# Spectral filter and feed-forward kernel: batch 0's first transform stage from stationary x into on-chip memory, batch 1's y set up later, and the inverse stage's calls in pairs inside the feed-forward

## The chip, the cores and the metric

The kernel runs on one core of a Trainium2 chip. The metric is device time in microseconds (us) of one execution; three runs are shown for the kernel before, and one more execution was profiled. The engines are PE (matrix multiply; PEld is its weight load), DVE (vector), ACT (scalar), POOL and SP, whose queue issues all DMAs here.

## The reference, cut to what matters

```python
B, S, D, FF = 8, 3136, 256, 1024
X = rfft(x, axis=1)                          # along the 3136 positions
Yr = Xr @ w_r - Xi @ w_i + b_r
Yi = Xr @ w_i + Xi @ w_r + b_i
Y  = soft_threshold(Yr, 0.01) + 1j * soft_threshold(Yi, 0.01)
y  = irfft(Y, n=3136, axis=1)
h  = relu(y @ w_in)                          # (B, S, 1024)
c  = conv_w[0]*h[s-1] + conv_w[1]*h[s] + conv_w[2]*h[s+1]   # per channel
out = (h * sigmoid(c)) @ w_out               # (B, S, 256)
```

## The kernel before, in words

**Spectral part.** A transform of 3136 = 49 x 64 points is two short transforms. Stage 1 (`quarters`, L296 to L301) multiplies x by the 49-point table `f1`: the table is the stationary operand (49 x 64), x streams past it 512 columns at a time, and row halves and column halves of the array work at once, four matmuls to a call. For batch 0 this is `stage1_head` (L320): eight pieces of x are loaded, multiplied, copied out of PSUM by ACT and DVE (L330, L331) and stored to a scratch tensor in DRAM, `sc1` (`store_a1`, L307 and L308). `load_a2` (L339) reads them back in the layout of the next stage. The other batches' stage 1 (`stage1`) runs between the items below. Then come 50 items: six per batch, each of four of the 24 frequency groups, and two for the left-over frequency of four batches each. For an item, stage 2 (`stage2`, L354, into `ps_s2`) is the 64-point transform; `mix` (L382, into `ps_mx`) multiplies by the complex weights `wmix`, which are written as high and low fp32r parts (`split`, L188 and L189); `threshold` and `stage3` (L416) follow, and the result `z1` is stored to a second scratch tensor, `sc2` (L421). The loop over `it` at L496 interleaves stage 2 of item `it` with the mix of `it-1`, the threshold of `it-2` and stage 3 of `it-3`. In it the order on PE, DVE and ACT is the written one.

**Stage 4** (`stage4`, L136) is the last inverse transform. Eight calls make a batch's `y`, each from a loaded tile `z2` (L133): 32 small fp32 matmuls with `z2` (50 x 64) stationary and the table `i2` (49 columns) streaming (L144), then ACT writes the high part `yh` (L150) and DVE the low part `yl` (L152). A call's PSUM tile comes from the pool `psh`, which has two buffers and is shared with the feed-forward. Batch 0's eight calls are woven into the end of the spectral part (`to_y`).

**Feed-forward.** 28 column blocks (`ci`) of 2 x 448 positions by 8 channel groups (`f`) make 224 steps. Step `st` runs `up` (L599): 12 matmuls of 450 columns into a `psh` tile; then the chain relu (ACT, L601), first tap (ACT L606, or DVE L604 for `f` 0 and 4), two more taps (DVE, L608), sigmoid (ACT, L609), product (DVE, L610), high part `gh` (ACT, L613) and low part `gl` (DVE, L614). Four steps later `down` (L627) multiplies them by `w_out`: 21 matmuls of 256 columns. While a batch is in the feed-forward, the next batch's `y` is made: `new_y` (L155) takes the buffer `y_a` or `y_b` and clears its edge columns with four small DVE memsets (L159, L160), and the steps with `f` of 1, 4 and 7 each run one stage 4 call behind their `up`. In the feed-forward, the Tile scheduler and not the written order decides how the instructions of each engine are lined up. `y_b`, batch 1's buffer, lies where `z1` tiles lay, so its first use waits for their stores.

Of the kernel before, what the change touches and what calls it, by code (L numbers as in the profile page):

```python
# [9 lines left out]
F32 = mybir.dt.float32  # L10
# [90 lines left out]
def spectral_ffn_kernel(ctx: ExitStack, tc: tile.TileContext, x, w_r, w_i, b_r, b_i,  # L101
# [10 lines left out]

    i2 = cst.tile([P, 112], F32, name="i2")[:, 0:R]
    cw = cst.tile([P, 3, NF], F32, name="cw")
    win = [cst.tile([P, NT, FF], F32R, name=f"win_{q}") for q in range(2)]
    wout = [cst.tile([P, NF, D], F32R, name=f"wout_{q}") for q in range(2)]
    small = cst.tile([P, 32], F32, name="small")
    mlam, warm = small[:, 0:1], small[:, 1:2]

# [43 lines left out]
    with ExitStack() as late:  # L163
# [6 lines left out]
        pool("top", 1, late, side="right").tile([P, 80], F32, name="pad")  # L170
        cmx = late.enter_context(tc.tile_pool(name="cmx", bufs=1, side="right"))
        DB, XRB, SL_ENG = 1, 3, nc.gpsimd
        ps1 = ps_early.enter_context(tc.tile_pool(name="ps1", bufs=2, space=PSUM))
        ps2 = ps_early.enter_context(tc.tile_pool(name="ps2", bufs=2, space=PSUM))
        psa = late.enter_context(tc.tile_pool(name="psa", bufs=1, space=PSUM, side="right"))
        psm = late.enter_context(tc.tile_pool(name="psm", bufs=1, space=PSUM, side="right"))

        f1 = c1.tile([P, P], F32, name="f1")[:, 0:SP]
        t2 = c1.tile([KQ, U + 1, K2], F32, name="t2")
        cmx.tile([P, 72], F32, name="pad")  # L180
# [13 lines left out]
        def load_t2(g):  # L194
            sl = slice(g * UG, min((g + 1) * UG, U + 1))
            return nc.sync.dma_start(t2[:, sl, :], fwd2v[:, sl, :])

        def load_mix():

            raw = [stg.tile([P, NT, D], F32, name=f"wm_raw{k}", tag="raw", bufs=2) for k in range(2)]  # L200
            for k in range(2):
                ld = nc.sync.dma_start(raw[k], (w_r, w_i)[k].rearrange("(t p) e -> p t e", p=P))
            yield ld
            split(wmix_hi[:, :, 0, :], wmix_lo[:, :, 0, :], raw[1])
            for k, op in ((1, ALU.subtract), (2, ALU.add)):
                w = stg.tile([P, NT, D], F32, name="wm", tag="wm")
                nc.vector.tensor_tensor(w, raw[0], raw[1], op=op)
                split(wmix_hi[:, :, k, :], wmix_lo[:, :, k, :], w)
            yield None

# [50 lines left out]
        def later():  # L261
            nc.sync.dma_start(i2, inv2)
            bits = [load_bits(conv_w[k].rearrange("(f p) w -> p f w", p=P), NF, "cw") for k in range(2)]
            for k in range(3):
                top, rest = yield from from_bits(bits[k], NF, "cw")
                yield nc.vector.tensor_tensor(cw[:, k, :], top, rest, op=ALU.add)
                if k == 0:
                    bits.append(load_bits(conv_w[2].rearrange("(f p) w -> p f w", p=P), NF, "cw"))
            pieces = []
            for t in range(NT):  # L270
                for c in range(0, FF, WP):
                    pieces.append(([q[:, t, c:c + WP] for q in win], winv[:, t, c:c + WP, :], "win"))
            for f in range(0, NF, 2):
                pieces.append(([q[:, f:f + 2, :].rearrange("p a d -> p (a d)") for q in wout], woutv[:, f:f + 2, :, :], "wout"))
            asked = []
            for n in range(len(pieces) + 1):
                work = split_weight(*asked.pop(0)) if n else iter(())
                for _ in range(5):
                    if n:
                        yield next(work)  # L280
                if n < len(pieces):
                    dst, src, nm = pieces[n]
                    asked.append((dst, load_bits(src, WP, nm), WP, nm))
                    yield None
                yield from work
# [10 lines left out]
        def quarters(ps, xr):  # L296

            for c in range(2):
                for h in range(2):
                    rows = slice(h * SP, h * SP + R)  # L300
                    nc.tensor.matmul(ps[h][c * SP:(c + 1) * SP], f1[rows, :], xr[rows, 2 * c:2 * c + 2, :], start=True, stop=True)  # L301

        def store_a1(b, jc, a1):

            to = sc1[b].rearrange("(w h) (q c j) d -> q c w h j d", h=2, c=2, j=2)[jc]
            for c in range(2):
                nc.sync.dma_start(to[c, 0:R - 1], a1[c * SP:c * SP + R - 1])  # L307
            return nc.sync.dma_start(to[:, R - 1], a1[R - 1::SP])  # L308
# [11 lines left out]
        def stage1_head(xs, b=0):  # L320

            with tc.tile_pool(name="ha", bufs=1, side="right", reuse_waits="tile") as ha:
                for jc, xr in enumerate(xs):
                    a1 = ha.tile([P, 2, JC // 2, D], F32, name=f"ha{jc}")
                    if jc % 2:
                        ps = [psm.tile([P, JC // 2, D], F32, name="ps_s1h", tag=f"ps_mx{h}") for h in range(2)]
                    else:
                        ps = [ps1.tile([P, JC // 2, D], F32, name="ps_s1") for h in range(2)]
                    quarters(ps, xr)
                    nc.scalar.copy(a1[:, 0], ps[0])  # L330
                    nc.vector.tensor_copy(a1[:, 1], ps[1])  # L331
                    st = store_a1(b, jc, a1)
            return st

        def load_a2(b, g):
# [107 lines left out]
        with tc.tile_pool(name="hx", bufs=1, side="right", reuse_waits="tile") as hx:
            xh = []
            for p in range(NQ):
                xr, ld = load_x(hx, 0, p, tag=f"hx{p}")
                xh.append(xr)
            with tc.issue_after(ld.ins):
                mix_w = load_mix()
                next(mix_w)  # L450
                load_t2(0)
                with tc.manual_schedule(engines={mybir.EngineType.PE, mybir.EngineType.DVE, mybir.EngineType.Activation}):
                    st = stage1_head(xh)
                    next(mix_w)
        asked = []

        def ask():
            asked.append(load_x(s1p, *firsts[NQ + len(asked)], bufs=XRB)[0])
# [5 lines left out]
                    ask()  # L464

        first = halves()
        with tc.issue_after(st.ins):
            a2s[0], ld = load_a2(*items[0])
        with tc.issue_after(ld.ins):
            ask()  # L470
            load_bias()
            a2s[1], ld = load_a2(*items[1])
            for _ in range(2):
                ask()
        order.enter_context(tc.manual_schedule(engines={mybir.EngineType.PE}))
        order.enter_context(tc.issue_after(ld.ins))
        io, cab, wk, wkf = [pool(nm, n, late, side="right") for nm, n in (("io", 3), ("cab", 1), ("wk", 2), ("wkf", 2))]
# [18 lines left out]
        for it in range(n_it + 1):  # L496
# [153 lines left out]
    for st in range(n_st + LAG):  # L650
        if st < n_st:
            ci, f = divmod(st, NF)
            hv = [divmod(2 * ci + a, NH) for a in range(2)]
            if f == 0:
                nb = hv[1][0] + 1
                if nb < B and nb not in ys and hv[0][0] == hv[1][0]:
                    ys[nb] = new_y((y_a, y_b)[nb % 2])
                    todo = [(nb, jg) for jg in range(NPC)]
            gs[st] = up(f, [(ys[b], a * CH) for b, a in hv])
            if todo and f in (1, 4, 7):  # L660
                b, jg = todo.pop(0)
                for _ in stage4(load_z2(zio, b, jg), jg, ys[b], psh.tile([P, 2, 512], F32, name="ps_s4", tag="ps_h")):
                    pass
        if st >= LAG:
            ci, f = divmod(st - LAG, NF)
            accs = down(ci, f, gs.pop(st - LAG), accs)
# [24 lines left out]
```

## Time and profile before

| | |
|---|---|
| median of three runs | 1700.11 us (1698.52 to 1700.85) |
| profiled execution | 1701.23 us |
| its span | 1699.5 us |
| PE busy | 1652.3 us, 97% of the span |
| DVE busy | 1470.4 us, 87% |
| ACT busy | 1208.4 us, 71% |
| feed-forward starts | at about 507.6 us |

A busy PE is not PE at its peak: matmuls overlap, and their recorded durations are longer than the distance from one start to the next. So the distances between starts are what a step costs, and the gaps in PE's row of time are where an engine order or a wait costs something.

### The profile page before, as it was taken

To read this page: it belongs to the slowest core of one execution; us is meant where nothing else is said; L and a number is where in the kernel's file an instruction comes from. 1 tells how busy PE (TensorE), PEld (TensorE's weight loads), DVE (VectorE), ACT (ScalarE), POOL (GpSimd) and SP (SyncE) were. 2 spreads that over 40 slices of the span, in tenths; PEclk is the share of its full clock that TensorE was granted. 3 is DMA by queue.
4 is the path that set the end of the run, shared out by engine and by line. 5 is a ranking of instruction groups with operands and counts; after the bars stand their busy time and mean duration, and the time that the engine had idled before them with its cause. 6 is when DMAs were issued, how large, how long until landed. Compare 5 with 4: busy or idle time off the path is not lost.

```text
span 1699.5 us, 35829 instructions
## 1 busy us (share of the span) xinstructions
PE 1652.3 (97%) x15200; PEld 1517.6 (89%) x15200; DVE 1470.4 (87%) x1757; ACT 1208.4 (71%) x1615; POOL 119.2 (7%) x54
## 2 busy tenths in 40 slices
PE   4899999999998999999999999999999999999998
PEld 1688888889987999999999999999999999999998
DVE  2698999999987888888888888888888888888887
ACT  1677777787666776777777677777777777777676
POOL 0122222222220000000000000000000000000000
PEclk9999999999998999999999999999999999999999
DMA  8998879785542110111111011111101111000001
GB/s 202 252 273 274 253 222 280 241 249 185 163 137 62 49 51 22 52 51 43 49 51 46 22 52 52 42 52 51 43 23 52 52 42 52 23 23 23 22 23 44
DMA packets 143361, 165.91 MB, mean 98 GB/s; under 512 B 11745, under 2 KB 115169, under 8 KB 143201
## 3 DMA queue, kind: packets, MB, share of 16 engines
q1 hardware_dynamic: 143200, 163.63, 33.2%
q8 instruction: 119, 1.95, 0.5%
q14 instruction: 42, 0.34, 0.1%
HBM read 86.00 MB, written 77.59 MB: 96 GB/s over the span
## 4 chain that ended last, share of the span: by engine, by line
PE 92%; DMA 2%; DVE 2%; SPq 2%; issue 1%; ACT 1%; POOL 0%; POOLq 0%; DVEq 0%; ACTq 0%
PE acc L627 33%; PE ps_h L599 32%; PE ps_mx L382 11%; PE ps_s L354 5%; PE ps_s L144 4%; PE ps_s L416 4%; PE ps_s L301 3%; DMA a<-sc 1%; DMA xr<-in_x_dram 1%; SPq L307 1%; POOL sl L404 0%; DMA sc<-z 0%; SPq L292 0%; DVE v L390 0%; DVE v L401 0%
## 5 line engine op out<-in xcount | busy, mean ns | idle before, releaser
L627 PE MATMUL acc<-wout,gh 128*128 128x256 f32 x3136 | 568.7, 281 | 8.5 <-ACT gh L613 8.5
L599 PE MATMUL ps_h<-yh,win 128*128 128x450 f32 x1792 | 550.3, 368 | 0.0
L608 DVE SCALAR_TENSOR_TENSOR c<-h,cw,c 128x896 f32<-128x896 f32 x448 | 513.2, 1147 | 28.2 <-ACT c L606 25.9
L627 PEld LDWEIGHTS acc<-wout,gh 128*128 128x128 f32 x3136 | 491.6, 188 | 17.3 <-ACT gh L613 8.8
L627 PE MATMUL acc<-wout,gl 128*128 128x256 f32 x1568 | 436.8, 280 | 0.0
L599 PEld LDWEIGHTS ps_h<-yh,win 128*128 128x128 f32 x1792 | 339.3, 189 | 25.9
L601 ACT ACTIVATE h<-ps_h 128x900 f32<-128x900 f32 x224 | 207.2, 925 | 208.7 <-PE ps_h L599 208.7
L599 PE MATMUL ps_h<-yl,win 128*128 128x450 f32 x896 | 329.8, 368 | 0.3 <-DVE yl L152 0.3
L610 DVE TENSOR_TENSOR c<-h,c 128x896 f32<-128x896 f32 x224 | 243.9, 1089 | 71.9 <-ACT c L609 71.4
L627 PEld LDWEIGHTS acc<-wout,gl 128*128 128x128 f32 x1568 | 293.6, 188 | 0.1
L614 DVE TENSOR_TENSOR gl<-c,gh 128x896 fp32r<-128x896 f32 x224 | 243.1, 1088 | 40.2 <-ACT gh L613 39.4
L609 ACT ACTIVATE c<-c 128x896 f32<-128x896 f32 x224 | 214.0, 955 | 62.0 <-DVE c L608 61.0
L613 ACT CAST gh<-c 128x896 fp32r<-128x896 f32 x224 | 211.7, 945 | 61.2 <-DVE c L610 60.8
L599 PEld LDWEIGHTS ps_h<-yl,win 128*128 128x128 f32 x896 | 169.5, 189 | 11.9 <-DVE yl L152 0.7
L606 ACT ACTIVATE c<-h,cw 128x896 f32<-128x896 f32 x168 | 175.2, 1043 | 1.8
L382 PE MATMUL ps_mx<-wmix_hi,fh 128*128 128x256 f32 x600 | 172.5, 287 | 0.6 <-DVE v L390 0.6
L382 PE MATMUL ps_mx<-wmix_hi,fl 128*128 128x256 f32 x600 | 172.2, 287 | 0.6 <-DVE fl L364 0.6
L382 PE MATMUL ps_mx<-wmix_lo,fh 128*128 128x256 f32 x600 | 167.7, 280 | 0.0
L404 POOL TENSOR_TENSOR sl<-v,sh 128x1024 fp32r<-128x1024 f32 x50 | 119.0, 2381 | 385.4 <-PE ps_s L416 189.9
L382 PEld LDWEIGHTS ps_mx<-wmix_hi,fl 128*128 128x128 f32 x600 | 113.0, 188 | 33.7 <-issue 32.5
L390 DVE TENSOR_TENSOR v<-ps_mx,p 64x512 f32<-64x512 f32 x200 | 137.2, 686 | 2.9
L354 PEld LDWEIGHTS ps_s<-t,a 128*128 128x128 f32 (+1 forms) x800 | 96.6, 197 | 39.2 <-issue 29.5
(83 smaller groups left out, 1766.0 us busy)
## 6 DMA issues: line engine op xcount, KB each, us to landing
z<-sc SPq DMA_DIRECT2D x128, 200.0 KB
xr<-in_x_dram SPq DMA_DIRECT2D x128, 192.0 KB
a<-sc SPq DMA_DIRECT2D x48, 512.0 KB
sc<-z SPq DMA_DIRECT2D x48, 512.0 KB
out_dram<-o SPq DMA_DIRECT2D x27, 896.0 KB
sc<-a SPq DMA_DIRECT2D x112, 192.0 KB
sc<-ha SPq DMA_DIRECT2D x16, 192.0 KB
win_bits<-in_moe_w_in_dram SPq DMA_DIRECT2D x4, 512.0 KB
```

The costliest lines, as they stand in the source:

```text
L354: nc.tensor.matmul(ps[:, k], a2[0:rows, k, t * P:(t + 1) * P], t2[0:rows, u, :], start=(k == 0), stop=(k == UG - 1), skip_group_check=True)
L382: nc.tensor.matmul(ps[c][:, k, :], lt, rh, start=(n == 0), stop=(n == len(mm) - 1))
L390: nc.vector.tensor_tensor(v[dst, :, k, :], ps[c][src], p1[src, c], op=ALU.add)
L599: nc.tensor.matmul(ps[:, a, 0:CH + 2], lt, rh, start=(n == 0), stop=(n == len(mm) - 1))
L601: nc.scalar.activation(h, ps[:, :, 0:CH + 2], AF.Relu)
L606: nc.scalar.mul(c, h[:, :, 0:CH], cw[:, 0, f:f + 1])
L608: nc.vector.scalar_tensor_tensor(c, h[:, :, k:k + CH], cw[:, k, f:f + 1], c, op0=ALU.mult, op1=ALU.add)
L609: nc.scalar.activation(c, c, AF.Sigmoid)
L610: nc.vector.tensor_tensor(c, h[:, :, 1:CH + 1], c, op=ALU.mult)
L613: nc.scalar.copy(gh, c)
L614: nc.vector.tensor_tensor(gl, c, gh.bitcast(F32), op=ALU.subtract)
L627: nc.tensor.matmul(acc[m // 2][:, m % 2, :], lt[:, sl], rh[:, f, :], start=(f == 0 and n == 0 and m % 2 == 0), stop=(f == NF - 1 and n == ...
```

## The change

It has three parts, and a few moves that come with them.

1. **Batch 0's stage 1.** `load_x0` loads all of x[0] as `xh`, with 49 rows on partitions twice (once for each half of the 256 channels) and 64 x 128 values in a row, in pieces of 512 bytes: nine DMAs. The new `stage1_head` has x stationary (49 x 64, its 64 columns 512 bytes apart) and the table's 49 columns streaming: eight groups of 32 small fp32 matmuls (L338) into four PSUM buffers of the temporary pool `psx`. From each group ACT (L342) and DVE (L343) make two copies each into `a0`, which stays on chip in the layout that stage 2 reads. `load_a2` returns a slice of `a0` for batch 0; the store to `sc1` and the six loads back go, except for one small store of the left-over frequency. `a0` takes the memory of `win` and `wout`, now one tile `ffw` that is claimed later. Two additions for `wmix` go from DVE to POOL (L203), and the splits of `wmix` now stand behind `stage1_head`'s copies.
2. **Batch 1's y.** `new_y` for it is called in step 3 instead of step 0.
3. **Pairs.** Stage 4 calls come two at a time, in the steps with `f` of 1 and 5.

```diff
-    win = [cst.tile([P, NT, FF], F32R, name=f"win_{q}") for q in range(2)]
-    wout = [cst.tile([P, NF, D], F32R, name=f"wout_{q}") for q in range(2)]
+    a0 = cst.tile([P, U + 1, D], F32, name="a0", tag="ffw", bufs=1)
...
-                nc.vector.tensor_tensor(w, raw[0], raw[1], op=op)
+                nc.gpsimd.tensor_tensor(w, raw[0], raw[1], op=op)
...
+        def load_x0(hx):
+            xr = hx.tile([P, R2, P], F32, name="xh")
+            xv = x[0].rearrange("(n j) (r d) -> r n j d", j=R2, r=2)
+            nc.sync.dma_start(xr[R - 1::SP], xv[:, R - 1])
+            for j in range(0, R2, 16):
+                for r in range(2):
+                    ld = nc.sync.dma_start(xr[r * SP:r * SP + R - 1, j:j + 16], xv[r, 0:R - 1, j:j + 16])
+            return xr, ld
+        def stage1_head(xr, psx):
+            to = a0.rearrange("p u (r c g i) -> c g p r u i", r=2, c=2, g=8)
+            for g in range(8):
+                ps = psx.tile([P, 2, 512], F32, name="ps_x")
+                for i in range(8):
+                    for r in range(2):
+                        rows = slice(r * SP, r * SP + R)
+                        for c in range(2):
+                            nc.tensor.matmul(ps[c * SP:(c + 1) * SP, r, i * R:(i + 1) * R], xr[rows, :, c * SP + 8 * g + i], f1[rows, 0:R],
+                                             start=(i == 0), stop=(i == 7), skip_group_check=True)
+                for c in range(2):
+                    src = ps[c * SP:(c + 1) * SP, :, 0:8 * R].rearrange("p r (i w) -> p r w i", w=R)
+                    nc.scalar.copy(to[c, g, 0:SP], src[:, :, 0::2])
+                    nc.vector.tensor_copy(to[c, g, SP:P, :, 0:U], src[:, :, 1::2])
...
-            if f == 0:
+            if f == (3 if ci == 0 else 0):
                 nb = hv[1][0] + 1
                 if nb < B and nb not in ys and hv[0][0] == hv[1][0]:
                     ys[nb] = new_y((y_a, y_b)[nb % 2])
                     todo = [(nb, jg) for jg in range(NPC)]
...
-            if todo and f in (1, 4, 7):
-                b, jg = todo.pop(0)
-                for _ in stage4(load_z2(zio, b, jg), jg, ys[b], psh.tile([P, 2, 512], F32, name="ps_s4", tag="ps_h")):
-                    pass
+            if todo and f in (1, 5):
+                two = [stage4(load_z2(zio, b, jg), jg, ys[b], psh.tile([P, 2, 512], F32, name="ps_s4", tag="ps_h")) for b, jg in todo[:2]]
+                todo = todo[2:]
+                for _ in range(3):
+                    for q in two:
+                        next(q, None)
```

**Order at the feed-forward's start.** On DVE before, behind batch 0's last `yl` (`y` of batch 0 is yh_6144 and yl_6145, of batch 1 yh_6610 and yl_6611; `c` and `h` belong to the first steps):

```order
L152 TENSOR_TENSOR yl_6145<-ps_s4_6538,yh_6144 128x2x49x8
L159 MEMSET yh_6610 128x2
L160 MEMSET yh_6610 128x2
L159 MEMSET yl_6611 128x2
L160 MEMSET yl_6611 128x2
L604 TENSOR_SCALAR c_6631<-h_6629,cw_77 128x896
L608 SCALAR_TENSOR_TENSOR c_6631<-h_6629,cw_77,c_6631 128x896 x2
```

On DVE after, at the same place (batch 1's `y` is yh_6850 and yl_6851):

```order
L153 TENSOR_TENSOR yl_6310<-ps_s4_6703,yh_6309 128x2x49x8
L160 MEMSET yh_6850 128x2
L161 MEMSET yh_6850 128x2
L160 MEMSET yl_6851 128x2
L161 MEMSET yl_6851 128x2
L619 TENSOR_SCALAR c_6790<-h_6788,cw_77 128x896
L623 SCALAR_TENSOR_TENSOR c_6790<-h_6788,cw_77,c_6790 128x896 x2
```

Though the call is written three steps later, the scheduler has left the memsets of batch 1's `y` ahead of the first step's first tap. On the SP queue before, up to the last store of `z1` (z1_6529; `z2` are stage 4's tiles):

```order
L421 DMA sc2_7_72<-z1_6406 128x1024
L133 DMA z2_6959<-sc2_1_66 50x8x128 x2
L133 DMA z2_7089<-sc2_1_66 50x8x128 x2
L133 DMA z2_7271<-sc2_1_66 50x8x128 x2
L421 DMA sc2_7_72<-z1_6529 128x1024
```

And after:

```order
L433 DMA sc2_7_72<-z1_6571 128x1024
L134 DMA z2_7216<-sc2_1_66 50x8x128 x2
L134 DMA z2_7220<-sc2_1_66 50x8x128 x2
L134 DMA z2_7486<-sc2_1_66 50x8x128 x2
L433 DMA sc2_7_72<-z1_6694 128x1024
```

The last store still stands behind three tiles of batch 1. 

**Order around a pair.** Step 89 (`ci` 11, `f` 1) on DVE before, from step 88's second group of taps on (step 87's `c` and `gl` are c_11577 and gl_11584, step 88's c_11629 and gl_11636, step 89's c_11675):

```order
L608 SCALAR_TENSOR_TENSOR c_11629<-h_11627,cw_77,c_11629 128x896
L614 TENSOR_TENSOR gl_11584<-c_11577,gh_11583 128x896
L608 SCALAR_TENSOR_TENSOR c_11675<-h_11673,cw_77,c_11675 128x896
L610 TENSOR_TENSOR c_11629<-h_11627,c_11629 128x896
L608 SCALAR_TENSOR_TENSOR c_11675<-h_11673,cw_77,c_11675 128x896
L152 TENSOR_TENSOR yl_11609<-ps_s4_11688,yh_11608 128x2x49x8
```

On DVE after, in the same step (step 88's `c` is c_11794, step 89's c_11840; the pair's tiles are ps_s4_11853 and ps_s4_11857):

```order
L623 SCALAR_TENSOR_TENSOR c_11794<-h_11792,cw_77,c_11794 128x896
L629 TENSOR_TENSOR gl_11749<-c_11742,gh_11748 128x896
L623 SCALAR_TENSOR_TENSOR c_11840<-h_11838,cw_77,c_11840 128x896
L625 TENSOR_TENSOR c_11794<-h_11792,c_11794 128x896
L623 SCALAR_TENSOR_TENSOR c_11840<-h_11838,cw_77,c_11840 128x896
L153 TENSOR_TENSOR yl_11774<-ps_s4_11853,yh_11773 128x2x49x8
L629 TENSOR_TENSOR gl_11801<-c_11794,gh_11800 128x896
L625 TENSOR_TENSOR c_11840<-h_11838,c_11840 128x896
L153 TENSOR_TENSOR yl_11774<-ps_s4_11857,yh_11773 128x2x49x8
```

The first `yl` of the pair stands where the single one stood. On PE after, the same step:

```order
L614 MATMUL ps_h_11825<-yh_9951,ffw_2163 128x450
L145 MATMUL ps_s4_11853<-i2_76,z2_11850 64x49 x32
L145 MATMUL ps_s4_11857<-i2_76,z2_11854 64x49 x32
L642 MATMUL acc0_11610<-ffw_2163,gh_11656 128x256 x2
...
L614 MATMUL ps_h_11947<-yh_9951,ffw_2163 128x450
```

Before, one call (ps_s4_11688) stood between that step's `up` and `down`. With two buffers in `psh`, the pair's first tile takes the one that the step's own `up` left free, and the second the one of that `up`, once its relu has read it; so the next step's `up` (ps_h_11947) now takes the buffer of the pair's first tile, where before it took that of the last `up`.

More of the change, by code (lines that the diff above doesn't have):

```diff
@@ L114, in spectral_ffn_kernel @@
     cw = cst.tile([P, 3, NF], F32, name="cw")
-    win = [cst.tile([P, NT, FF], F32R, name=f"win_{q}") for q in range(2)]
-    wout = [cst.tile([P, NF, D], F32R, name=f"wout_{q}") for q in range(2)]
+    FW = NT * FF
+    a0 = cst.tile([P, U + 1, D], F32, name="a0", tag="ffw", bufs=1)
+    win, wout = [], []
     small = cst.tile([P, 32], F32, name="small")
@@ L172, in spectral_ffn_kernel @@
         DB, XRB, SL_ENG = 1, 3, nc.gpsimd
[L173 to L176, printed above, removed]
         f1 = c1.tile([P, P], F32, name="f1")[:, 0:SP]
@@ L269, in later @@
             pieces = []
+            ffw = cst.tile([P, 4 * FW], F32R, name="ffw", tag="ffw", bufs=1)
+            win[:] = [ffw[:, q * FW:(q + 1) * FW].rearrange("p (t f) -> p t f", t=NT) for q in range(2)]
+            wout[:] = [ffw[:, (2 + q) * FW:(3 + q) * FW].rearrange("p (f d) -> p f d", f=NF) for q in range(2)]
             for t in range(NT):
@@ L318, in stage1, with load_a2 @@
             yield None
[L320 to L335, printed above, removed]
+        def load_x0(hx):
[20 more added lines that the diff above has]
+                    nc.vector.tensor_copy(to[c, g, SP:P, :, 0:U], src[:, :, 1::2])
+        def load_a2(b, g, ld):
+            if b == 0 and g < NG:
+                return a0[:, g * UG:(g + 1) * UG], ld
             a2 = a2p.tile([KQ, UG, D], F32, name="a2")
@@ L442, in spectral_ffn_kernel @@
         load_f1()
[L443 to L447, printed above, removed]
+        with tc.tile_pool(name="hx", bufs=1, side="right", reuse_waits="tile") as hx, \
+                tc.tile_pool(name="psx", bufs=4, space=PSUM, reuse_waits="tile") as psx:
+            xh, ld = load_x0(hx)
+            with tc.issue_after(ld.ins):
+                ld = load_t2(0)
             with tc.issue_after(ld.ins):
                 mix_w = load_mix()
+                ld = next(mix_w)
+            with tc.manual_schedule(engines={mybir.EngineType.PE, mybir.EngineType.DVE, mybir.EngineType.Activation}):
+                stage1_head(xh, psx)
                 next(mix_w)
[L451 to L454, printed above, removed]
+        ps1 = ps_early.enter_context(tc.tile_pool(name="ps1", bufs=2, space=PSUM))
+        ps2 = ps_early.enter_context(tc.tile_pool(name="ps2", bufs=2, space=PSUM))
+        psa = late.enter_context(tc.tile_pool(name="psa", bufs=1, space=PSUM, side="right"))
+        psm = late.enter_context(tc.tile_pool(name="psm", bufs=1, space=PSUM, side="right"))
         asked = []
@@ L466, in spectral_ffn_kernel @@
         first = halves()
-        with tc.issue_after(st.ins):
-            a2s[0], ld = load_a2(*items[0])
         with tc.issue_after(ld.ins):
@@ L471, in spectral_ffn_kernel @@
             load_bias()
-            a2s[1], ld = load_a2(*items[1])
             for _ in range(2):
                 ask()
+        a2s = {n: load_a2(*items[n], ld)[0] for n in range(2)}
         order.enter_context(tc.manual_schedule(engines={mybir.EngineType.PE}))
@@ L521, in spectral_ffn_kernel @@
                     i1s[it] = load_inv1(it)
+            if it == 2:
+                nc.sync.dma_start(sc1[0][4 * U:K1].rearrange("q j d -> (q j) d"), a0[0:R2, U])
             some(two, 2)
@@ L559, in spectral_ffn_kernel @@
             if it + 2 < n_it:
-                a2s[it + 2], ld = load_a2(*items[it + 2])
+                a2s[it + 2], ld = load_a2(*items[it + 2], ld)
         some(to_y(1), 2)
```

## The prediction

> **What bounds the kernel.** I read the page first, then PE's waits, then PE in order of time. PE is the bound:
>
> ```profile
> span 1699.5 us, 35829 instructions
> PE 1652.3 (97%) x15200; PEld 1517.6 (89%) x15200; DVE 1470.4 (87%) x1757; ACT 1208.4 (71%) x1615; POOL 119.2 (7%) x54
> ```
>
> The waits of PE (total us, times, longest) say where the missing 3% is:
>
> ```profile
> PE ps_s L354 <- DMA a<-sc: 18.3, 2, 17.8
> PE acc L627 <- ACT gh L613: 8.5, 1, 8.5
> PE ps_s L354 <- DMA i_raw<-in_inv_dram: 5.3, 1, 5.3
> PE ps_s L301 <- DMA xr<-in_x_dram: 5.2, 1, 5.2
> ```
>
> Three stand in the first 51 us (batch 0's way through DRAM), one where the feed-forward starts. Elsewhere PE never waits long, so what the change adds there is paid in full.
>
> **Part 1, the head.** PE in order of time (start, us, line, what; in brackets the idle time before):
>
> ```profile
> 9.81 2.14 PE L301 MATMUL ps_s<-xr,f 49*64 49x512 f32 x8
> 11.94 2.10 PE L301 MATMUL ps_s1h<-xr,f 49*64 49x512 f32 x8
> 40.23 3.75 PE L354 MATMUL ps_s<-t,a 128*128 128x128 f32 x16 [17.84 <-DMA a<-sc]
> 43.91 1.83 PE L301 MATMUL ps_s<-xr,f 49*64 49x512 f32 x8
> 51.03 3.75 PE L354 MATMUL ps_s<-t,a 128*128 128x128 f32 x16 [5.29 <-DMA i_raw<-in_inv_dram]
> 54.44 0.56 PE L382 MATMUL ps_mx<-wmix_hi,fh 128*128 128x256 f32 x1
> 56.13 1.09 PE L301 MATMUL ps_s<-xr,f 49*64 49x512 f32 x8
> ```
>
> Before, mix 0 starts at 54.44, and from there PE runs on. The change removes the round trip: 24 stores and six loads. What must come ahead of mix 0 now is a chain.
>
> (a) *x lands.* The bytes are the same 3.21 MB. Windows of the load and of a stretch where most transfers are `z2` tiles (512-byte pieces); the last two columns are the DMA share and GB/s:
>
> ```profile
> 2.00:16.00 14.00, 10.13 (x40) 2.06 (x40) 2.77 (x4) 2.56 (x6) 0.00 (x0) 1.00 0.98 209
> 496.00:520.00 24.00, 18.73 (x484) 16.11 (x475) 9.27 (x14) 12.82 (x16) 4.28 (x2) 1.00 0.80 200
> ```
>
> At 209 GB/s x needs 15.4 us from 2.0; at the second row's 200/0.80 = 250 GB/s it needs 12.8. New is that the first matmul needs all of it. I take 17.5, between 15 and 23 (the pieces at three quarters of 209).
>
> (b) *256 small matmuls.* They are like stage 4's, 32 to a group:
>
> ```profile
> 502.38 2.08 PE L144 MATMUL ps_s<-i,z 50*64 50x49 f32 x128
> 504.40 0.38 PE L416 MATMUL ps_s<-sh,i_hi 128*128 128x256 f32 x1
> 505.73 1.15 PE L144 MATMUL ps_s<-i,z 50*64 50x49 f32 x64
> 506.81 0.39 PE L416 MATMUL ps_s<-sh,i_hi 128*128 128x256 f32 x1
> ```
>
> A call costs 506.81 - 505.73 = 1.08 us from start to start. But the first stage's groups of eight go every 2.13 us at 9.81 and take 1.09 at 56.13, a factor of 1.95, though PE had nothing else between them for twelve microseconds: in small tiles the head stays at half rate (the granted clock reads 1.00 in the window row above; the starts decide). So 2.1 per group, 16.9 for eight. The new stationary is read 512 bytes apart; no row shows such a read. Its bound below is no cost, above a doubled group (4.2); I take none, since half rate leaves time between the loads.
>
> (c) *Copies.* Grouped rows of the first 60 us (mean ns):
>
> ```profile
> L316 ACT COPY a<-ps_s 128x512 f32<-128x512 f32 x4 | 2.1, 590 | 2.5 <-PE ps_s L301 2.5
> L357 ACT COPY d<-ps_s 128x256 f32<-128x256 f32 x4 | 1.5, 373 | 22.1 <-PE ps_s L354 22.1
> L360 DVE TENSOR_TENSOR fl<-ps_s,fh 128x512 fp32r<-128x512 f32 x4 | 2.7, 680 | 0.0
> L359 DVE TENSOR_TENSOR d<-ps_s,d 128x256 f32<-128x256 f32 x4 | 1.7, 424 | 22.1 <-ACT fh L358 22.1
> ```
>
> Between 256 and 512 values, 400 cost ACT 0.49 and 384 cost DVE 0.55. The two read one PSUM tile in turn (ACT, DVE, ACT, DVE), 2.3 us with the hand-overs; the next group's first copy overlaps, so a period is about 1.9, under 2.1. Only the last 2.3 counts.
>
> So `a0` is ready at 17.5 + 16.9 + 2.3 = 36.7. Then stage 2 of item 0 (3.75, half rate), a stage 1 group (1.83) and stage 2 of item 1, which needs no DMA now (1.9 at full rate: the rows from 51.03 on gain full rate after 4.6 us). Mix 0 starts at 36.7 + 7.9 = 44.6, counting 0.4 for the `wmix` splits, which now stand here. It then skips the half-rate start that costs 0.7 at 54.44. Gain 54.4 + 0.7 - 44.6 = **10.5**; by the ends of (a) 5 to 13. The two additions on POOL are hidden by the matmuls; the small store and the later loads by mix 0. `ffw` is first written after item 5: nothing.
>
> **Part 2, batch 1's y.** At the feed-forward's start:
>
> ```profile
> 512.43 1.14 SPq L421 DMA_DIRECT2D sc<-z  x1
> 519.28 0.06 DVE L159 MEMSET yl<- 128x2 f32 x1 [10.39 <-DMA sc<-z]
> 522.40 0.95 ACT L609 ACTIVATE c<-c 128x896 f32<-128x896 f32 x1 [7.06 <-DVE c L608]
> 525.50 2.07 PE L627 MATMUL acc<-wout,gh 128*128 128x256 f32 x8 [8.47 <-ACT gh L613]
> ```
>
> The memset holds DVE until the last store of `z1` lands at 519.2, and PE pays 8.5 us. By the order rows the memset still stands ahead of the first tap, and the store still behind three `z2` tiles, so DVE goes on at 519.3 again. What changes is PE's order: five `up`s come before the first `down`, where it was three and a stage 4 call. The third `up` is through when relu 2 (behind sigmoid 0, to 523.3) frees a buffer for the fifth at 524.2, 1.3 us earlier than 525.5, and by then PE has four `up`s behind it (9.8 us) instead of three and a call (8.6). Sum -2.5, with the restart in half rate both times; **-2.9** with the pair's saving here. The ends: nothing, and -11 if the wait were gone.
>
> **Part 3, pairs.** A single call costs a step 984.45 - 978.25 = 6.20 less the plain 989.40 - 984.45 = 4.95, 1.25 us:
>
> ```profile
> 978.25 0.37 PE L599 MATMUL ps_h<-yh,win 128*128 128x450 f32 x1
> 980.81 1.15 PE L144 MATMUL ps_s<-i,z 50*64 50x49 f32 x64
> 981.89 0.50 PE L627 MATMUL acc<-wout,gh 128*128 128x256 f32 x2
> 984.45 0.37 PE L599 MATMUL ps_h<-yh,win 128*128 128x450 f32 x1
> 989.40 0.37 PE L599 MATMUL ps_h<-yh,win 128*128 128x450 f32 x1
> ```
>
> The x128 row above goes on to its follower after 504.40 - 502.38 = 2.02, so the second call adds 0.94 instead of 1.25; less 0.05, since it waits for the relu of its step's `up`. Of 28 pairs the order sets 21 back to back: -21 x 0.25 = -5.3.
>
> Against that stands PSUM. The next `up` now needs the buffer of the pair's first tile, hence its `yl`. This is the same step on ACT and DVE:
>
> ```profile
> 980.92 0.92 ACT L601 ACTIVATE h<-ps_h 128x900 f32<-128x900 f32 x1 [2.33 <-PE ps_h L599]
> 984.36 0.91 ACT L150 CAST yh<-ps_s 128x784 fp32r<-128x784 f32 x1
> 983.71 1.15 DVE L608 SCALAR_TENSOR_TENSOR c<-h,cw,c 128x896 f32<-128x896 f32 x1
> 984.77 1.09 DVE L610 TENSOR_TENSOR c<-h,c 128x896 f32<-128x896 f32 x1
> 985.77 1.15 DVE L608 SCALAR_TENSOR_TENSOR c<-h,cw,c 128x896 f32<-128x896 f32 x1
> 986.84 0.97 DVE L152 TENSOR_TENSOR yl<-ps_s,yh 128x784 fp32r<-128x784 f32 x1
> ```
>
> `yl` ends at 987.81, 7.00 after the call's start; nobody waited. With a pair, the next `up` would start at 984.45 + 0.99 = 985.44, and waits 2.4 us. The order after decides it, pair by pair. Where `yl` comes behind tap, product, tap, as here: in steps 89 and 145 2.4 each, in step 33 1.5 (eight more `down` matmuls of 0.117 lie between). In steps 9, 13 and 37 the same sequence without a `gl` ahead of it starts 0.9 earlier: 1.4 at step 37, 1.2 at 13 with two more `down`s; step 9 comes while DVE is still behind from 519, and I give it 2. In fourteen pairs `yl` comes before the second tap and the product, so it ends two instructions (1.06 + 1.01 of spacing, 983.71 to 985.77) and more earlier, at some 4.1 after the start, 0.6 before it is needed: nothing. Seven pairs are split by five `down`s: no saving, 0.1 of wait each. Sum 2.4 + 2.4 + 1.5 + 1.4 + 1.2 + 2 + 0.7 = +11.6. The ends: 0, if ACT and DVE catch up, and 16, if the fourteen lose their 0.6 and 0.3 more. Net of part 3: **+6.3**.
>
> **Sum.** -10.5 - 2.9 + 6.3 = -7.1. The profiled execution took 1701.23, 1.1 over the median; on the median, 1700.1 - 7.1 = **1693**.
>
> **Rivals.** *Wait for nothing:* DVE is idle often enough to run `yl` early, and part 3 is -5.3. For it: DVE is 87% busy. Against: the 7.00 is measured, in the order that the pairs keep. -10.5 - 2.9 - 5.3 gives 1681.
>
> *Strided weights, the slower side:* the group at 4.2 makes the head 33.6, mix 0 starts at 61.4, 6.3 later than before; 1710. From 3.4 per group on the head gains nothing. For it: nothing in the rows, as they have no such read. The Trainium skill ("SBUF — State Buffer", the note on SBUF cachelines) says that an access which leaves its 16-byte line pays; no trace here shows it for a weight load, and it names no price.
>
> *The head at full rate:* activity raises the rate within the head. Then the copies' 1.9 sets the period, the head takes 1.9 x 8 + 1.1, some 0.6 less, and stage 2 of item 0 costs 1.9 instead of 3.75: 1690.5. Against: 9.81 to 22 us at 2.13. The Trainium skill ("TensorE: Matmul & The Clock Gate", Part 1) gives this rule, full clock after some 3.4 us of sustained activity; the rows of 51.03 agree with 4.6, those of 9.81 do not, and by the rule alone the sum would be this rival's.
>
> *The change does what it says in part 2:* the store lands before DVE asks. 6.7 us of wait and 2 of half rate go: 1684. Against: the SP order, with the DMAs 80% busy there.
>
> *Gain eaten in the head:* x at 23 instead of 17.5, 1698.5.
>
> **Numbers.** The sum as worked out 0.45 (1688 to 1698), waits for nothing 0.15, strided weights 0.12, full rate 0.10, part 2 0.06, gain eaten 0.12. The range 1682 to 1703 leaves out strided weights and half of the waits-for-nothing case. 0.2% (3.4 us) is about what a measurement can tell from no change. Faster: 0.38 of the first, 0.15, 0.09, 0.06: 0.68. Same: 0.07, 0.09 and 0.01: 0.17. Slower 0.15.
>
> **What would show it.** Right: one burst of 64-row matmuls from about 17 us, `ps_x` groups 2.1 apart, mix 0 near 45; a memset still waiting some 10 us for a store; PE waits of 1 to 2.5 us on `yl` in about six `up`s, none in the others. Wrong: groups at 1.1 or 4 us; no wait at the memset; or waits on `yl` in nearly all pairs or none.

## The result, and the profile after

The changed kernel takes 1718.9 us (median of four runs, 1718.5 to 1719.8), the kernel before in the same session 1700.5. The ratio is 1.0111 with a 95% interval of 1.0098 to 1.0124: 18.4 us slower, where 7 us faster was forecast. The page of the profile after begins:

```profile
span 1716.7 us, 36745 instructions
PE 1657.1 (97%) x15648; PEld 1538.6 (90%) x15648; DVE 1477.8 (86%) x1763; ACT 1215.1 (71%) x1623; POOL 121.7 (7%) x56
```

Busy shares hardly moved. What moved are PE's waits (total us, times, longest):

```profile
PE ps_x L338 <- DMA xh<-in_x_dram: 24.6, 2, 22.7
PE ps_h L614 <- DVE yl L153: 11.6, 11, 2.2
PE ps_s L145 <- ACT h L616: 7.4, 12, 1.2
PE ps_h L614 <- ACT h L616: 4.5, 1, 4.5
PE ps_s L366 <- issue: 2.3, 1, 2.3
```

The waits of 18.3 and 5.3 before (batch 0's round trip through DRAM, and one put down to the load of a table) are gone, and 24.6 for x stands in their place and in that of the 5.2 for x before. The second and third row are new but for 0.3 us at 507.1, where the feed-forward starts; that was there before too. So with the pairs PE waits 11.3 on `yl`, in ten places, and 7.4 on relu, in twelve.

**The head.** First SP's queue, then PE in order of time:

```profile
1.96 14.21 SPq L326 DMA_DIRECT2D xh<-in_x_dram  x8
16.21 2.28 SPq L192 DMA_DIRECT2D t<-in_fwd_dram  x1
22.73 0.53 PE L338 MATMUL ps_x<-f,xh 49*64 49x49 f32 x4 [22.73 <-DMA xh<-in_x_dram]
25.16 18.93 PE L338 MATMUL ps_x<-f,xh 49*64 49x49 f32 x508 [1.89 <-DMA xh<-in_x_dram]
46.41 3.75 PE L366 MATMUL ps_s<-t,a 128*128 128x128 f32 x16 [2.32 <-issue]
53.21 0.37 PE L394 MATMUL ps_mx<-wmix_hi,fh 128*128 128x256 f32 x1
```

SP needs 14.2 us to issue the eight large transfers of x, and the last piece lands at 25.2. The eight groups take 18.9, the last copies 2.3, and mix 0 starts at 53.21, only 1.2 ahead of the 54.44 before.

**The transition.** The memset still waits on DVE for a store, and PE for the relu behind it, 4.5 us instead of 8.5, restarting at 520.9 instead of 525.5:

```profile
515.97 0.06 DVE L160 MEMSET yl<- 128x2 f32 x1 [8.90 <-DMA sc<-z]
520.91 0.74 PE L614 MATMUL ps_h<-yh,ffw 128*128 128x450 f32 x1 [4.50 <-ACT h L616]
```

**A pair whose `yl` is late** (step 89, PE, then ACT and DVE):

```profile
983.44 2.23 PE L145 MATMUL ps_s<-i,z 50*64 50x49 f32 x128
990.49 0.47 PE L614 MATMUL ps_h<-yh,ffw 128*128 128x450 f32 x1 [2.17 <-DVE yl L153]
986.99 0.91 ACT L151 CAST yh<-ps_s 128x784 fp32r<-128x784 f32 x1
987.40 1.08 DVE L625 TENSOR_TENSOR c<-h,c 128x896 f32<-128x896 f32 x1
988.41 1.15 DVE L623 SCALAR_TENSOR_TENSOR c<-h,cw,c 128x896 f32<-128x896 f32 x1
989.47 0.97 DVE L153 TENSOR_TENSOR yl<-ps_s,yh 128x784 fp32r<-128x784 f32 x1
```

`yh` is written at 987.9, but DVE has a product and a tap ahead of `yl`, which ends at 990.44, 7.00 us after the first call's start. The next `up` begins 0.05 later.

**A pair whose relu is late** (the second call needs the buffer of its own step's `up`):

```profile
1183.38 1.15 PE L145 MATMUL ps_s<-i,z 50*64 50x49 f32 x64
1185.65 1.15 PE L145 MATMUL ps_s<-i,z 50*64 50x49 f32 x64 [1.12 <-ACT h L616]
1183.84 0.94 ACT L628 CAST gh<-c 128x896 fp32r<-128x896 f32 x1 [1.65 <-DVE c L625]
1184.68 0.92 ACT L616 ACTIVATE h<-ps_h 128x900 f32<-128x900 f32 x1
```

ACT stands idle for 1.65 us with `gh` at the head of its queue, waiting for DVE's product, and the relu that PE needs is queued behind it.

**Half rate.** Behind its start, the feed-forward has three places at which the granted clock (last but two) falls:

```profile
555.00:560.00 5.00, 4.91 (x83) 4.82 (x84) 5.00 (x6) 4.29 (x6) 0.00 (x0) 0.66 0.65 153
1290.00:1295.00 5.00, 2.85 (x11) 2.42 (x11) 5.00 (x6) 3.23 (x4) 0.00 (x0) 0.82 0.54 99
1295.00:1300.00 5.00, 5.00 (x31) 4.72 (x31) 2.55 (x3) 2.37 (x3) 0.00 (x0) 0.84 0.00 0
1490.00:1495.00 5.00, 5.00 (x75) 4.93 (x68) 5.00 (x6) 4.06 (x6) 0.00 (x0) 0.66 0.01 3
```

By these shares it is some 3.4 us at a clock of 0.50 each time, and each costs about 1.6 us: behind 1292.5, `up`'s matmuls go every 0.37 us, and otherwise every 0.21. PE had just waited 1.18 us (at 555.1), 2.15 (at 1292.5) and 1.12 (at 1489.6). The longest wait, 2.17 at 990.5, has no fall behind it (1.00 from 990 to 1000), so the length of the wait alone doesn't decide it. What does stays open.

### The profile page after: what moved, and what is told of

It reads as the page before. It is cut to its first block, busy times and chain, and to the rows that moved or that the text cites. A ratio compares the mean times of both kernels' runs of the same rounds, so it can differ in the third digit from the quotient of the medians.

```text
span 1716.7 us, 36745 instructions
## 1 busy us (share of the span) xinstructions
PE 1657.1 (97%) x15648; PEld 1538.6 (90%) x15648; DVE 1477.8 (86%) x1763; ACT 1215.1 (71%) x1623; POOL 121.7 (7%) x56
## 4 chain that ended last, share of the span: by engine, by line
PE 71%; DVE 16%; ACT 8%; issue 3%; DMA 1%; SPq 1%; POOLq 0%; POOL 0%; DVEq 0%; ACTq 0%
PE ps_h L614 23%; PE acc L642 23%; PE ps_mx L394 11%; DVE c L623 7%; PE ps_s L366 5%; PE ps_s L428 4%; PE ps_s L300 3%; DVE c L625 3%; ACT h L616 3%; ACT c L621 2%; DVE gl L629 2%; ACT gh L628 2%; DVE yl L153 2%; PE ps_x L338 1%; PE ps_s L145 1%
## 5 line engine op out<-in xcount | busy, mean ns | idle before, releaser
L642 PE MATMUL acc<-ffw,gh 128*128 128x256 f32 x3136 | 568.6, 281 | 0.0
L614 PE MATMUL ps_h<-yh,ffw 128*128 128x450 f32 x1792 | 551.5, 370 | 15.9 <-DVE yl L153 11.3
L642 PEld LDWEIGHTS acc<-ffw,gh 128*128 128x128 f32 x3136 | 496.4, 189 | 8.2
L642 PE MATMUL acc<-ffw,gl 128*128 128x256 f32 x1568 | 438.8, 281 | 0.0
L614 PEld LDWEIGHTS ps_h<-yh,ffw 128*128 128x128 f32 x1792 | 340.6, 190 | 44.5 <-DVE yl L153 13.7
L614 PE MATMUL ps_h<-yl,ffw 128*128 128x450 f32 x896 | 330.9, 369 | 0.3 <-DVE yl L153 0.3
L642 PEld LDWEIGHTS acc<-ffw,gl 128*128 128x128 f32 x1568 | 295.2, 189 | 0.5
L614 PEld LDWEIGHTS ps_h<-yl,ffw 128*128 128x128 f32 x896 | 170.1, 190 | 11.8 <-DVE yl L153 0.7
L394 PEld LDWEIGHTS ps_mx<-wmix_hi,fh 128*128 128x128 f32 x600 | 113.1, 188 | 1.4 <-PE ps_mx L394 0.7
```

What stands on the lines that cost most here:

```text
L394: nc.tensor.matmul(ps[c][:, k, :], lt, rh, start=(n == 0), stop=(n == len(mm) - 1))
L614: nc.tensor.matmul(ps[:, a, 0:CH + 2], lt, rh, start=(n == 0), stop=(n == len(mm) - 1))
L642: nc.tensor.matmul(acc[m // 2][:, m % 2, :], lt[:, sl], rh[:, f, :], start=(f == 0 and n == 0 and m % 2 == 0), stop=(f == NF - 1 and n == ...
```

## The experiments

Each ratio is taken to runs of the kernel before that were made beside the experiment; their medians lie between 1699.4 and 1700.7 us. A single profile can lie some us from the median of its kernel, so times are compared by medians, and profiles only within a place.

**A. Each part alone.** `pairs_only` puts the change's pair loop into the kernel before:

```diff
-            if todo and f in (1, 4, 7):
-                b, jg = todo.pop(0)
+            if todo and f in (1, 5):
+                two = [stage4(...) for b, jg in todo[:2]]
...
```

> The kernel before with part 3 alone: stage 4's calls in pairs at f 1 and 5 instead of one each at f 1, 4 and 7. Theory 1 (the pairs carry the loss: the next `up` waits for the first tile's `yl`, and the second call waits for the relu of its own step, because two buffers of PSUM hold `up` and both calls): after's waits of PE on `yl` (11.6 us) and on relu (7.4), some 3 us at half rate behind the longest of them, less 21 x 0.17 = 3.6 saved. 1716 to 1721 us, 16 to 20 above before, PE waits on `yl` 10 to 13 and on relu 6 to 8 in the feed-forward. Theory 2 (the new first stage, or batch 1's later y, shifts the work of ACT and DVE, and the waits come from that shift): the pairs alone cost under 6 us, 1700 to 1706. Theory 3 (the prediction's own price): +6.3, 1707.

1725.7 us, ratio 1.0146 [1.0132, 1.0159]: +25.2, over theory 1's 16 to 20. PE's waits are 13.6 on `yl` and 5.6 on relu, each just outside its range. The pairs alone lose more than the whole change does.

`no_pairs` takes them out of the changed kernel:

```diff
-            if todo and f in (1, 5):
+            if todo and f in ((3, 5, 7) if ci == 0 else (1, 4, 7)):
```

> The changed kernel with part 3 undone: single calls at f 1, 4 and 7, in the first chunk at 3, 5 and 7, as batch 1's y is set up at f 3 there. Parts 1 and 2 stay. Theory 1: the head's 1.8 us and some 1 to 3 of the transition are left as gain, 1695 to 1699 us; no wait on `yl` over 0.3 in the feed-forward. Theory 2 (the loss comes from parts 1 and 2): 1710 or more.

1697.8 us, ratio 0.9981 [0.9972, 0.9989]; no wait on `yl` over 0.4 us in the feed-forward, as theory 1 said. So the pairs cost 21.1 us within the change.

`head_only` is part 1 alone (`no_pairs` with `new_y` at `f == 0` and calls at 1, 4, 7).

> The kernel before with part 1 alone: batch 0's first stage with x stationary and `a0` on chip, the y of batch 1 and the single calls as before. Theory 1: mix 0 starts at 53.2 as after, the feed-forward starts 1.8 us earlier, the rest as before with its 8.5 us at the transition: 1698 to 1699.5. Theory 2 (the head costs later what it saves at the start, by the order of DVE or by SBUF): 1702 or more.

1699.4 us, ratio 0.9994 [0.9985, 1.0002]: 1.2 less, which the interval doesn't separate from nothing.

`y_later_only` is part 2 alone:

```diff
-            if f == 0:
+            if f == (3 if ci == 0 else 0):
```

> The kernel before with part 2 alone: batch 1's y set up at f 3 of the first chunk, single calls there at f 3, 5 and 7, else at 1, 4 and 7. Theory 1 (five `up`s ahead of the first `down` cover a part of the memset's wait, which stays): PE's wait at the first `down` falls from 8.5 to between 4 and 6.5, 1697 to 1699.5. Theory 2 (the wait is only moved): 1700 to 1702. Theory 3 (the change does what it says, the store lands before the memset): no wait of DVE at the memset, 1692 to 1695.

1696.7 us, ratio 0.9983 [0.9971, 0.9996], between the ranges of theories 1 and 3. PE's wait at the first `down` is nearly gone (its row of the waits), but the memset's is not (DVE in order of time; this trace names no releaser):

```profile
PE acc L627 <- ACT gh L613: 0.8, 1, 0.8
```

```profile
519.00 0.06 DVE L159 MEMSET yl<- 128x2 f32 x1 [6.18 <-issue]
```

In this execution the feed-forward also began late, at 512.2 (507.6 before), so less of the wait was left to see. In `head_only`, which leaves part 2 out, the same wait was short too:

```profile
PE acc L642 <- ACT gh L628: 2.9, 1, 2.9
```

So these profiles don't give part 2 its size. The median carries the verdict: part 2 gains 2.9 us by the ratio, 0.7 to 4.9 by its interval. Alone, the three parts come to 25.2 - 1.2 - 3.8 = +20.2 by medians, the whole change to +18.4.

**B. What the pairs wait for.** `yl_off_psum` frees the pair's tile earlier:

```diff
-        nc.vector.tensor_tensor(view(y[1]), src, view(y[0].bitcast(F32)), op=ALU.subtract)
+        nc.vector.tensor_tensor(view(y[1]), view(y[0].bitcast(F32)) if off else src, view(y[0].bitcast(F32)), op=ALU.subtract)
```

> The changed kernel, but in the feed-forward `yl` is computed from `yh` alone, in an instruction of the same size that reads SBUF and not the PSUM tile; so the pair's tile is free after ACT's `yh`. It leaves out the `yl` part of batches 1 to 7. Theory 1 (the tile held for `yl` is what the next `up` waits for): PE's 10.6 us of waits on `yl` and part of the 3 us at half rate go, the waits for relu (7.4) stay: 1704 to 1709 us. Rival a (PE waits because ACT and DVE as a whole are behind; freeing the tile only moves the wait to `yh`, relu or `gh`): 1714 or more, with as many us of PE waits under another name.

1720.9 us, no faster than the change (ratio to before 1.0112 [1.0096, 1.0128]). Theory 1 fell, and rival a stands. The waits on `yl` in the feed-forward (11.3) are gone, and those on relu went from 7.4 to 17.1. The row of the waits, and PE, ACT and DVE around one of them:

```profile
PE ps_s L145 <- ACT h L616: 17.1, 16, 2.6
```

```profile
709.22 1.96 PE L145 MATMUL ps_s<-i,z 50*64 50x49 f32 x64 [2.40 <-ACT h L616]
707.41 0.94 ACT L628 CAST gh<-c 128x896 fp32r<-128x896 f32 x1 [1.65 <-DVE c L625]
708.25 0.92 ACT L616 ACTIVATE h<-ps_h 128x900 f32<-128x900 f32 x1
706.29 1.08 DVE L625 TENSOR_TENSOR c<-h,c 128x896 f32<-128x896 f32 x1
```

It is the pattern of 1183 above: PE waits for relu, relu stands behind `gh`, `gh` waits for DVE's product. So the tile was only where PE met the delay. The next theory put the cause on DVE, to which a pair brings two `yl` at once. `no_yl` leaves them out:

```diff
-        nc.vector.tensor_tensor(view(y[1]), src, view(y[0].bitcast(F32)), op=ALU.subtract)
+        if not off:
+            nc.vector.tensor_tensor(view(y[1]), src, view(y[0].bitcast(F32)), op=ALU.subtract)
```

> The changed kernel, but in the feed-forward a pair's two `yl` instructions are left out (a memset on POOL fills `yl` with zeros once a batch), so DVE has two times 0.97 us less to do at each pair, and the tiles are free after `yh`. It leaves out the `yl` part of batches 1 to 7. Theory 2 (the relu that frees the buffer stands on ACT behind a `gh` or sigmoid that waits for DVE, and a pair's two `yl` at once put DVE behind): the 17 us of PE's waits on relu, which stood there when only the tile was freed, fall under 5, 1698 to 1706 us. Theory 3 (ACT's own order, its two `yh` and the relu, with two buffers for three tiles, is enough for the waits): 10 us or more of relu waits stay, 1712 to 1721.

1706.7 us, ratio 1.0035 [1.0022, 1.0048], just over the upper end of theory 2. The pairs' waits fall to four, 5.6 us where theory 2 gave under 5 (PE's waits):

```profile
PE ps_s L145 <- ACT h L617: 5.6, 4, 2.8
PE ps_h L615 <- ACT h L617: 5.5, 1, 5.5
```

The second row is the transition. From 18.7 (11.3 on `yl` in the feed-forward and 7.4 on relu) to 17.1 by the tile, and from 17.1 to 5.6 by DVE's work: most of the waiting is DVE's load at the pair. `no_yl` also takes work from DVE as a whole; but in `no_pairs` DVE has all the `yl` to do, one at a time, and PE doesn't wait for it. What remains is ACT's order or the two buffers; no run gave the pool a third. The scheduler lines up the feed-forward anew for each kernel, so these runs compare whole orders and not one instruction.

**C. The head.** `x_halves` (from `no_pairs`) issues one half of the channels first and works on it first:

```diff
-            for j in range(0, R2, 16):
-                for r in range(2):
+            for r in range(2):
+                for j in range(0, R2, 16):
...
-                for i in range(8):
-                    for r in range(2):
-                        rows = slice(r * SP, r * SP + R)
+            for r in range(2):
+                rows = slice(r * SP, r * SP + R)
+                for g in range(0, 8, 2):
...
```

> No pairs, as in the experiment of that name, and the head goes by halves of D: the loads of the first half are issued ahead of the second's, the four groups of matmuls of the first half come first, with as many matmuls, copies and values in each as before. Theory 1 (the head is late because its first matmul waits for all of x): the first half lands near 14 us, half of the work is done when the second lands at 25, mix 0 starts 7 to 9 us earlier than 53.2: 1689 to 1691 us. Rival (the transfers of both halves share the queues and land together): mix 0 no more than 2 us earlier, 1696 to 1698.

1707.2 us, ratio 1.0034 [1.0022, 1.0047]: 9 slower than `no_pairs`, which neither theory had. PE starts earlier and never waits again, yet needs 36.9 us instead of 18.9:

```profile
17.91 36.93 PE L339 MATMUL ps_x<-f,xh 49*64 49x49 f32 x512 [17.91 <-DMA xh<-in_x_dram]
```

In the changed kernel neighbouring matmuls alternate between the row halves, and with them between the two halves of the PSUM tile; here many in a row use the same rows and the same half of the tile, and as many matmuls take twice as long. No run separates the two. The Trainium skill ("TensorEngine Tiling (Array Packing)", Tiling Modes) says that different tiles of the array can load and multiply in parallel; by these two rows the row halves do, if it is not the halves of the PSUM tile. So x in halves, as a theory on x's landing, was not tested fairly.

`x_contig` reads 64 neighbouring values as stationary; `x_32k` reads x in long pieces:

```diff
x_contig, the stationary operand:
- xr[rows, :, c * SP + 8 * g + i]
+ xr[rows, 48 + (8 * g + i) % 16, c * SP:(c + 1) * SP]
x_32k, the view of x that is loaded:
- xv = x[0].rearrange("(n j) (r d) -> r n j d", j=R2, r=2)
+ xv = x[0].rearrange("(n r j k) (h d) -> r n (j k h) d", r=2, j=16, k=2, h=2)
```

> No pairs, as in the experiment of that name, and in the head each stationary is 64 neighbouring values of x instead of 64 values 512 bytes apart, taken from the last rows that land; so the first stage of batch 0 computes something else. Theory a (the strided read costs the 0.27 us by which a group of 32 matmuls, 2.37, is over the 2.1 predicted): groups come every 2.1 us, the eight end 2 us earlier. Theory b (the read costs nothing, and the rest of 2.37 is the first group's start or the copies): 2.37 again. Theory c (at half rate the loads are hidden, and the rate would rise if the loads were shorter): 1.1 to 1.9.

> No pairs, as in the experiment of that name, and x of batch 0 is read into the same tile in the same 9 transfers, but each partition's part is one run of DRAM of 8 KB and more in place of pieces of 512 bytes; so the first stage of batch 0 computes something else. Theory a (the size of the pieces sets when x lands): the last piece lands at 17 to 18 us, as the 209 GB/s of the load before give, 7 us earlier than the changed kernel's 25.2. Theory b (the queue, the start, or all of x in 9 transfers sets it): 23 us or later.

Each ran once (1696.0 and 1694.6 us), too few to compare times, so their traces are read. PE in `x_contig`, the first stretch of the head until PE waits:

```profile
24.53 6.20 PE L338 MATMUL ps_x<-f,xh 49*64 49x49 f32 x219 [1.87 <-DMA xh<-in_x_dram]
```

The weight loads of the tile `ps_x` (least, median and most ns), in `x_contig` and in the changed kernel:

```profile
L338 PEld LDWEIGHTS ps_x<-f,xh x512: 175/223/228, 22.2 to 41.0; 49*64 49x64 f32 x171
```

```profile
L338 PEld LDWEIGHTS ps_x<-f,xh x512: 214/248/257, 22.7 to 43.7; 49*64 49x64 f32 x171
```

PE and SP's queue in `x_32k`:

```profile
22.49 18.97 PE L338 MATMUL ps_x<-f,xh 49*64 49x49 f32 x508 [1.67 <-DMA xh<-in_x_dram]
1.93 5.39 SPq L326 DMA_DIRECT2D xh<-in_x_dram  x8
```

Contiguous weights go at 6.20 x 64 / 219 = 1.81 us a group instead of 2.38 (a group is 64 instructions of PE). So the strided read has a price, 0.57 a group. That pace is in theory c's range, and not theory a's 2.1. Then PE waits three times, 2.0 us in all; the trace names no releaser, and the copies are the likely one. With these waits the eight groups take 2.1 us less, near the 2 that theory a gave.

Long pieces cut the issue time by 8.8, from 14.2 to 5.4 us, but x lands at 22.5, 2.7 earlier and not 7. So the issue time alone doesn't set the landing. The windows up to it, in the changed kernel and in `x_32k` (GB/s is last):

```profile
2.00:25.16 23.16, 0.54 (x5) 0.38 (x5) 0.00 (x0) 0.22 (x2) 0.00 (x0) 1.00 1.13 174
```

```profile
2.00:22.49 20.49, 0.53 (x4) 0.37 (x5) 0.00 (x0) 0.21 (x2) 0.00 (x0) 1.00 0.98 198
```

In both some 4.0 MB had moved by then, 0.8 more than x's 3.21: other transfers share the queues with it. The rate rose from 174 to 198 GB/s. So the size of the pieces is a part of the delay, and neither theory gave that number.

**D. The clock in the head.** `warm_head` and `warm_to_x` fill PE's idle time before x with 14 and 24 matmuls of zeros, in the best version below:

```diff
+                dm = hx.tile([P, 512], F32, name="dm")
+                nc.gpsimd.memset(dm, 0.0)
+                wp = psx.tile([P, 2, 512], F32, name="ps_x")
+                for _ in range(24):
+                    nc.tensor.matmul(wp[:, 0], dm[:, 0:P], dm, start=True, stop=True)
                 stage1_head(xh, psx)
```

> The version with head, later y, product edges and no pairs (1689.4), and 14 matmuls of zeros, 128x128 by 512 columns in fp32, which fill PE's idle time from 2 us until x has landed. Theory a (the head runs at half rate because PE starts it cold): the groups of 32 matmuls, 2.37 each before, come at 1.2 to 2.0 (the copies then set the pace, as they did with contiguous weights), the first stage 2 takes 1.9 instead of 3.75, mix 0 starts 4 to 7 us earlier: 1683 to 1686 us. Theory b (small tiles run at half rate in whatever state PE was before): the groups stay at 2.3 or fall back to it within some us, 1688 to 1691.

> As the experiment before it, with 24 matmuls of zeros instead of 14, so that PE has no idle time of over 2 us between them and the head. Theory a (the head is at half rate because PE starts it cold): groups of 32 at 1.2 to 2.0 us instead of 2.37, mix 0 at 46 to 50 instead of 53 to 54, 1683 to 1686 us. Theory b (small tiles fall to half rate from any state): the granted clock falls to 0.5 within some us of the head, groups at 2.2 or more, 1688 to 1691.

1690.9 and 1690.7 us, in theory b's range: no gain over 1689.4 and 1690.3 without them. In the first, PE had idled 8.2 us again before x came. The second starts the head at full clock, and shows it fall while PE is busy. First PE in order of time, then windows of the line (granted clock, DMA share and GB/s are last):

```profile
26.04 18.99 PE L344 MATMUL ps_x<-f,xh 49*64 49x49 f32 x508 [1.55 <-DMA xh<-in_x_dram]
```

```profile
26.10:28.10 2.00, 2.00 (x56) 2.00 (x60) 1.00 1.07 200
30.00:34.00 4.00, 4.00 (x117) 4.00 (x116) 0.50 0.66 166
38.00:42.00 4.00, 4.00 (x118) 4.00 (x116) 0.50 0.32 22
```

The pace is nearly the same at 1.00 (56 in 2 us) as at 0.50 (117 in 4 us): with `x_contig`, the strided weight loads set it, not the clock. The Trainium skill ("TensorE: Matmul & The Clock Gate", Part 1) gives full clock after some 3.4 us of sustained activity; here a busy row of small tiles went the other way.

**E. A version that beats both.** `memset_last` is part 2 with the memset taken out of DVE's way, `head_memset` adds part 1:

```diff
+            for at in (0, S + 1):
+                nc.vector.tensor_scalar_mul(q[:, :, at:at + 1], qf[:, :, S:S + 1], 0.0)
...
+                if jg == NPC - 1:
+                    zero(ys[b])
```

> Part 2 alone, as in the experiment of that name, and the edge columns of batches 1 to 7's y are set to zero by a product of the last column instead of a memset, so that they cannot be put ahead of stage 4's last call. Theory 1 (the memset's wait for the last store of `z1`, ahead of the first tap on DVE, sets the transition): DVE has no wait of 6 to 10 us there, PE none over 1 us at the first `down`s; 1692 to 1695 us, against 1696.7 with part 2 alone. Rival (`yh` or `yl` of the first call inherits the wait for the store, or PE was hardly held any more): 1696 to 1699.

> Parts 1 and 2 without pairs and with the edge columns set by a product, as in the experiments of those names: the candidate for a version that beats both. If the head's gain (1.1 alone) adds to 5.9 (part 2 with the edges): 1692.5 to 1695. If the transition absorbs it (DVE is behind either way): 1694.5 to 1697.

> The same version without matmuls of zeros, once more beside it: 1689 to 1691 us by either theory.

`memset_last` takes 1694.8, ratio 0.9959 [0.9944, 0.9973]; `head_memset` 1689.4 and 1690.3, ratios 0.9946 [0.9931, 0.9962] and 0.9942 [0.9929, 0.9954]: 9 to 10 us faster than before, and 29 faster than the change. The first is in theory 1's range; `head_memset` is under both of its own, and its interval overlaps that of `memset_last`, so what part 1 adds there is not settled. DVE's first tap in `head_memset` starts on the relu, no longer on a store, and PE has no wait over 0.4 us from 505 to 530 us:

```profile
510.80 0.69 DVE L625 TENSOR_SCALAR c<-h,cw 128x896 f32<-128x896 f32 x1 [2.96 <-ACT h L622]
```

## Why the prediction was wrong, step by step

The failing term is **part 3**, +6.3 in the sum and +21.1 in the runs: 14.8 of the 26 us between forecast and result. Its `yl` part came out right in size, 11.6 forecast and 11.3 measured, though by some luck. Five of the six steps named waited as forecast (89 and 145: 2.17 and 2.15 against 2.4; 33, 37 and 13: 1.24, 1.39 and 1.17 against 1.5, 1.4 and 1.2). Step 9, given 2, had none, and five of the seven split pairs waited 3.2 together where 0.1 each was given.

Three of its other numbers were not right. The relu wait was put at 0.05 a pair, some 1 us in all; it is 7.4 in twelve places, as the prediction looked at a step whose relu came early and did not ask what stands ahead of it on ACT. The saving was 0.25 a pair and is 0.17 (by the starts of the `up`s, a pair without a wait adds 2.33 us at step 93, and two single calls 2.50), 3.6 and not 5.3. Half rate in three places, some 4.8, was not in the sum. Together 11.3 + 7.4 + 4.8 - 3.6 = 19.9, and the transition waits 0.8 longer than in `no_pairs` (4.5 against 2.9 and 0.8 there): 20.7 against 21.1. It closes less well by the traces. From its first `up` to the end the feed-forward takes 1210.9 us in the profiled execution of the changed kernel and 1186.2 in that of `no_pairs`, 24.7 more, so some 4 us are in none of these terms.

The reason behind the sum was also too narrow: it treated the held buffer as the cause. By the experiments of B it is the place. With the buffer freed most of the time is lost one link further on, and only less work on DVE at the pair takes most of it away.

**Part 1** was forecast at -10.5 and gives -1.2. Step (a) failed: x lands at 25.2, outside the 15 to 23 given. The bytes of x alone were divided by 209 and 250 GB/s; the queues moved 174 until x had landed, and some 0.8 MB of it were other transfers, though all of x is needed before the first group. Step (b) took 2.1 a group, 16.9, by half rate, and no price for strided weights; it is 2.38, 18.9. With neighbours PE goes at 1.81 where it doesn't wait, so the 2.1 was too slow and the 0.57 of the strided read was missing; the two errors partly cancel. The rival "head at full rate" is dead, since full clock left the pace of the groups nearly as it was. Step (c), 2.3, was right, and the way from there to mix 0 took 6.8 instead of 7.9. The rival "gain eaten in the head" is what part 1 did.

**Part 2** was right: -2.9 forecast, a ratio of 0.9983 (2.9 us, with the wide interval above) measured, the memset still waiting for its store. In the changed kernel PE stops where the prediction had it, at the fifth `up`, for a relu; it goes on at 520.9 and not 524.2, as the store landed 3.3 us earlier than in the profile before. `memset_last` took the wait itself away, and with part 2 that was worth 5.9 us by medians, not the 11 of the prediction's lower end.

## What to carry to other kernels

- Two pieces of side work back to back save little on the engine that bounds the kernel, and ask the engines that feed it for twice as much at one time. Where these are 70 to 90% busy, look in their queues for what stands ahead of the instruction that frees a buffer, and for what that one waits for in turn.
- A wait on a buffer names the place and not the cause: free the buffer once, and see whether the time goes or moves.
- A load that one matmul needs whole costs its bytes at the rate of its own piece size, and what shares the queues; less issue time alone need not bring it sooner. A layout that makes the data fit may make the weight read strided; measure that by reading neighbours once.

## What was not expected of the hardware

- A stationary operand of 49 x 64 fp32 with its columns 512 bytes apart loads in 248 ns, and in 223 from neighbours; the groups took 2.38 and 1.81 us. The strided groups' pace was nearly the same at a granted clock of 1.00 and of 0.50.
- In a busy row of such matmuls the granted clock fell from 1.00 to 0.50 within some 4 us, and stayed there to the row's end 15 us later.
- Matmuls of 49 rows that alternate between the two row halves go at twice the rate of those that stay in one for many in a row (18.9 against 36.9 us for as many). The first alternate between two halves of a PSUM tile as well.
- The granted clock fell for some 3.4 us behind waits of PE of 1.12, 1.18 and 2.15 us, and not behind one of 2.17.
